# A new load path and a new step order for windowed attention with a gMLP: casting loads on one GpSimd queue, and constant matmuls in TensorE's early gaps

**Chip, cores, metric.** One core of a Trainium2 chip. The metric is the device time of one execution in microseconds (us), median of several runs; the profile gives a span that is about 2 us shorter than the time of the same execution. Engines in the profile: PE (TensorE matmul), PEld (its weight loads), DVE (VectorE), ACT (ScalarE), POOL (GpSimd), SP (SyncE); a name with a "q" is the engine's sequencer, which waits and issues. L12 is line 12 of the kernel in question, so the same step has different lines before and after.

## The reference, cut to what matters

```python
# attention: B, H, S, D = 4, 8, 768, 64; key j is kept for query i if j < 4 or 0 <= i - j < 128
scores = q @ k.T / sqrt(D);  a = softmax(where(keep, scores, -1e9));  x = heads_to_columns(a @ v)   # (4, 768, 512)
# gMLP on x: d_ff = 1024, u and v halves of 512
h = gelu_tanh(x @ w_in);  u, v = h[..., :512], h[..., 512:]
v_n = (v - mean) / sqrt(var + 1e-6) * g_ln
gated = u * (w_sg @ v_n + b_sg)            # w_sg: (768, 768), over the sequence
out = x + gated @ w_out                    # float32
```

## The kernel before

The program is one list of steps; each engine executes its own steps in that order. A step is a name with indices: `MK.0.0.2` is the mask of batch 0, head pair 0, third group of score blocks. What matters here:

```python
# loads: float32, issued from SyncE, then cast by GpSimd
def LQ(b, p):
    return nc.sync.dma_start(out=q32.new((b, p)), in_=q[b, 2*p:2*p+2].rearrange("h (p t) d -> p h (t d)", p=128))
def LV(b, p):                                   # rows of 64 floats
    return nc.sync.dma_start(out=v32.new((b, p))..., in_=v[b, 2*p:2*p+2].rearrange("h (t p) d -> p (h t) d", p=128))
def cast(dst, src):
    return nc.gpsimd.tensor_scalar(out=dst, in0=src, scalar1=1.0, scalar2=1.0, op0=ALU.mult, op1=ALU.mult)
# weights: cast by the DMA, issued from GpSimd
def LWS():
    return nc.gpsimd.dma_start(out=wsg_rows, in_=moe_w_sg.rearrange("(c p) f -> p c f", p=128))
# ... cut ...
HOLDS = "LQ.1.0<LWS LG<LWS"     # batch 1's loads wait until w_sg has landed

def transposes(name, ring, b, p):               # two heads = 128 columns in one transpose
    src = ring[b, p].rearrange("p t h d -> p t (h d)")
    ...
    for t in range(NT):
        nc.tensor.transpose(ps[:, t, :], src[:, t, :], iden)

def MK(b, p, g):                                # causal window of 128 on exp(scores)
    if g == 0 or (b == 0 and g not in MK0):
        nc.vector.tensor_mul(...)               # mask tile on VectorE
        return
    nc.gpsimd.affine_select(...)                # two selects on GpSimd
```

The steps of batch 0 end with the attention-times-v matmuls (`AV`), their normalization (`NR`), the transposes of x (`XT`, evicted by `XE`) and then the gMLP, whose first matmuls are the v-half of `x @ w_in` (`MV.0.*`). I call all that comes ahead of the first of these **the front**. After it, the gMLP of a batch and the attention of the next are interleaved.

The softmax here doesn't subtract the row's maximum and nothing guards it: scores larger than these inputs give would overflow.

## Time and profile before

| | before |
|---|---|
| time, median (range) | 173.68 us (172.44 to 173.81), 3 runs |
| span of the profile | 171.1 us |
| busy: PE, DVE, ACT, POOL | 151.1, 138.7, 101.9, 95.9 us |
| first v-half matmul starts | 33.5 us |
| w_in, w_sg, w_out have landed | 24.4, 32.0, 34.6 us |

The page's rows of digits are 40 slices of the span, each digit the busy share in tenths. "Chain" means the work that ended last, followed back from the end; each line is start, length, what. The lines themselves are in the prediction below.

### The profile page before, as it was taken

Reading aid. Unit: us, or ns where it says so; the run is one execution under the profiler, and the core shown is the slowest. Engines: PE = TensorE matmul, PEld = TensorE weight load, DVE = VectorE, ACT = ScalarE, POOL = GpSimd, SP = SyncE. Lnnn points to the kernel's source line nnn. Section 1 sums busy time; section 2 is a strip of 40 time slices with the busy share of each in tenths; the row PEclk is TensorE's granted clock in tenths of the full one; section 3 lists DMA queues with packets and bytes.
Section 4 is the critical chain, followed back from the end, with each engine's and each line's share of the span. In section 5 each row is a group of like instructions: output and inputs, shape, how many; then the busy total and the mean of one; then the engine's idle time right before and its main releaser. Section 6 shows DMA issues by size and latency. Waiting matters only on the chain.

```text
span 171.1 us, 3623 instructions
## 1 busy us (share of the span) xinstructions
PE 151.1 (88%) x1388; PEld 90.3 (53%) x1388; DVE 138.7 (81%) x290; ACT 101.9 (60%) x119; POOL 95.9 (56%) x158
## 2 busy tenths in 40 slices
PE   0447889699989899979999999999999999999970
PEld 0323568364655466645576565544565744556530
DVE  6198696629989999999999799848889994959962
ACT  0416887674995768956649985864997006860000
POOL 7789766013899999999599678043306400520000
PEclk9999999999999999999999999999999999999999
DMA  5999989999999999989999200970100374210044
GB/s 166 325 314 240 210 117 195 221 252 246 316 299 297 279 288 298 314 160 214 321 323 281 64 4 17 230 248 0 61 4 0 64 170 180 80 61 0 34 156 184
DMA packets 49617, 30.94 MB, mean 181 GB/s; under 512 B 35904, under 2 KB 46400, under 8 KB 49600
## 3 DMA queue, kind: packets, MB, share of 16 engines
q1 hardware_dynamic: 47072, 27.93, 61.5%
q0 software_dynamic: 2368, 2.75, 9.8%
q8 instruction: 11, 0.18, 0.4%
q10 hardware_dynamic: 160, 0.03, 0.1%
q14 instruction: 6, 0.05, 0.1%
HBM read 24.81 MB, written 6.29 MB: 182 GB/s over the span
## 4 chain that ended last, share of the span: by engine, by line
PE 63%; DVE 20%; ACT 5%; DMA 5%; POOL 3%; issue 2%; DVEq 0%; ACTq 0%
PE mm L466 15%; PE mm L483 11%; PE sc L446 10%; PE sc L399 10%; PE sc L310 5%; PE mm L266 4%; ACT P L318 3%; DVE qT L276 3%; DVE gtmp L471 3%; PE mm L350 3%; DVE x_sb L370 3%; DMA q<-in_q_dram 3%; DVE P L325 3%; DVE wsg_gated L476 2%; PE mm L356 2%
## 5 line engine op out<-in xcount | busy, mean ns | idle before, releaser
L318 ACT ACTIVATE P<-sc 128x1024 bf16<-128x1024 f32 (+1 forms) x48 | 43.7, 953 | 12.2 <-PE sc L310 10.6
L466 PE MATMUL mm<-wsgT,z 128*128 128x384 bf16 x192 | 34.0, 326 | 0.0
L329 POOL TENSOR_SCALAR_AFFINE_SELECT P<-P 128x512 bf16<-128x512 bf16 x28 | 20.1, 719 | 18.2 <-ACT P L318 13.8
L466 PEld LDWEIGHTS <-z 128*128 128x128 bf16 x192 | 18.0, 98 | 12.1 <-issue 1.2
L483 PE MATMUL mm<-w_out_sb,wsg_gated 128*128 128x512 bf16 x96 | 23.0, 379 | 1.1 <-DVE wsg_gated L476 1.1
L399 PE MATMUL sc<-w_in_sb,xT 128*128 128x512 bf16 x96 | 22.4, 379 | 0.2 <-ACT xT L384 0.2
L446 PE MATMUL sc<-xT,w_in_sb 128*128 128x384 bf16 x128 | 22.4, 326 | 0.0
L471 DVE SCALAR_TENSOR_TENSOR gtmp<-mm,g_sb,b_bc 128x384 bf16<-128x384 f32 x32 | 19.3, 611 | 3.6 <-PE mm L466 3.5
L487 DVE TENSOR_TENSOR ot<-mm,x_sb 128x512 f32<-128x512 f32 x24 | 16.1, 683 | 5.4 <-PE mm L483 5.3
L310 PE MATMUL sc<-qT,kT 64*128 64x256 bf16 x192 | 17.0, 287 | 3.8 <-DVE qT L276 1.7
L350 PE MATMUL mm<-v_sb,P 128*128 128x65 bf16 x192 | 18.0, 201 | 1.6 <-DVE P L325 1.4
L404 ACT ACTIVATE vt<-sc 128x1024 f32<-128x1024 f32 x12 | 12.3, 1024 | 11.7 <-PE sc L399 11.7
L182 POOL TENSOR_SCALAR q<-q 128x768 bf16<-128x768 f32 x16 | 14.3, 891 | 8.6 <-DMA q<-in_q_dram 8.6
L370 DVE TENSOR_TENSOR x_sb<-mm,rcp 128x384 bf16<-128x384 f32 x32 | 17.8, 557 | 1.1
L350 PEld LDWEIGHTS <-P 128*128 128x128 bf16 x192 | 15.2, 102 | 5.9 <-issue 2.1
L411 DVE BATCH_NORM_STATS2 st<-vt 128x6 f32<-128x512 f32 x24 | 16.2, 675 | 2.5 <-ACT vt L404 2.5
L325 DVE TENSOR_TENSOR P<-P,mask 128x1024 bf16<-128x1024 bf16 x20 | 16.4, 830 | 1.3 <-ACT P L318 1.1
L356 PE MATMUL mm<-v_sb,P 128*128 128x65 bf16 x160 | 16.9, 200 | 0.0
L446 PEld LDWEIGHTS <-w_in_sb 128*128 128x128 bf16 x128 | 12.4, 98 | 8.4
L281 ACT COPY kT<-mm 128x768 bf16<-128x768 bf16 x16 | 12.8, 801 | 5.6 <-PE mm L266 5.6
L182 POOL TENSOR_SCALAR v_sb<-v 128x768 bf16<-128x768 f32 x16 | 14.9, 937 | 1.9 <-DMA v<-in_v_dram 1.9
L418 POOL TENSOR_SCALAR rs<-mv 128x2 f32<-128x2 f32 x12 | 3.0, 251 | 22.6 <-DVE mv L412 22.2
(61 smaller groups left out, 253.8 us busy)
## 6 DMA issues: line engine op xcount, KB each, us to landing
q<-in_q_dram SPq DMA_DIRECT2D x16, 384.0 KB, 6.6
k<-in_k_dram SPq DMA_DIRECT2D x16, 384.0 KB, 5.8
v<-in_v_dram SPq DMA_DIRECT2D x16, 384.0 KB, 6.9
out_dram<-ot SPq DMA_DIRECT2D x24, 256.0 KB, 2.0
wsg_gated<-in_moe_w_sg_dram POOLq DMA_DIRECT2D x1, 1152.0 KB, 8.8
w_in_sb<-in_moe_w_in_dram POOLq DMA_DIRECT2D x2, 512.0 KB, 7.2
w_out_sb<-in_moe_w_out_dram POOLq DMA_DIRECT2D x1, 512.0 KB, 8.1
b_bc<-in_moe_b_sg_dram SPq DMA_DIRECT2D x1, 384.0 KB
```

The source lines that it names most:

```text
L182: return nc.gpsimd.tensor_scalar(out=dst, in0=src, scalar1=1.0, scalar2=1.0, op0=ALU.mult, op1=ALU.mult)
L310: nc.tensor.matmul(sc[:, hl, 256 * jl:256 * jl + n], kT[b, p][rows, 128 * j:128 * (j + 1)], qT[b, p][rows, 128 * j:128 * j + n], start=Tru ...
L318: nc.scalar.activation(out=pt[:, :, 0:w], in_=sc_ring[b, p, g][:, :, 0:w], func=AF.Exp, scale=scale)
L325: nc.vector.tensor_mul(pt[:, :, 0:w], pt[:, :, 0:w], m.unsqueeze(1).to_broadcast([128, 2, w]))
L350: nc.tensor.matmul(av[:, il, hl, :], P[b, p, i // 2][:, hl, 256 * (i % 2):256 * (i % 2) + 128], vb[:, h, i, :], start=first, stop=False)
L356: nc.tensor.matmul(av[:, il, hl, :], P[b, p, j // 2][:, hl, 256 * (j % 2) + 128:256 * (j % 2) + 256], vb[:, h, j, :], start=False, stop=False)
L370: nc.vector.tensor_mul(xs[:, 3 * half:3 * half + 3, 128 * p:128 * (p + 1)].rearrange("p t (h d) -> p t h d", h=2), av[:, :, :, 0:Dh], rcp. ...
L399: nc.tensor.matmul(hp[:, jl, :], xT[b][:, j, c, :], w_in_sb[:, c, d_half:2 * d_half], start=(c == 0), stop=(c == KD - 1))
L446: nc.tensor.matmul(hp[:, hf, 0:NH], w_in_sb[:, c, 128 * dc:128 * (dc + 1)], xT[b][:, 3 * hf:3 * hf + 3, c, :], start=(c == 0), stop=(c == ...
L466: nc.tensor.matmul(ps[:, 0:NH], z[b][:, si, 128 * dc:128 * (dc + 1)], wsgT[:, si, NH * hf:NH * (hf + 1)], start=(si == 0), stop=(si == NT ...
L471: nc.vector.scalar_tensor_tensor(out=gtmp.new((b, hf, dc)), in0=mm_ring["g", b, hf, dc][:, 0:NH], scalar=g_sb[:, dc:dc + 1], in1=b_bc[:, N ...
L483: nc.tensor.matmul(ps, gatedT[:, (2 * b + hf) % 3, dc, 128 * tl:128 * (tl + 1)], w_out_sb[:, dc, :], start=(dc == 0), stop=(dc == KU - 1))
```

## The change

Its intent: take the casts of q and k from GpSimd by letting the DMA cast them, put the large loads, all but the very first of q and k, in one queue in the order of need (so that SyncE's hold goes), keep TensorE's clock up in the front, and spread the evictions, masks and products anew over the engines. The core of the diff, cut:

```diff
-    def LQ(b, p):
-        return nc.sync.dma_start(out=q32.new((b, p)), ...)
+    def load(ring, src, b, i):                       # bfloat16 destination: the DMA casts
+        n = 2 if b == 0 else 4                       # heads per load
+        ...
+        return nc.gpsimd.dma_start(out=dst, in_=src[b, hs].rearrange("h (p t) d -> p h (t d)", p=128))
+    def rows(eng, ring, src, b, p):                  # v, float32
+        return eng.dma_start(out=ring.new((b, p))..., in_=src[b, 2*p:2*p+2]...)
     def LV(b, p):
-        return nc.sync.dma_start(...)
+        return rows(nc.sync if b in DT else nc.gpsimd, v32, v, b, p)      # DT = ()
-HOLDS = "LQ.1.0<LWS LG<LWS"
+HOLDS = "LG<LWS"
+    def HM(n):                                       # n constant matmuls ahead of the next PSUM tile's use
+        pre[0] = n
+    def fresh(ring, key):
+        t = ring.new(key)
+        for _ in range(pre[0]):
+            nc.tensor.matmul(..., iden, ks_sink[1][:, 0:512], start=True, stop=True)
     for t in range(NT):
-        nc.tensor.transpose(ps[:, t, :], src[:, t, :], iden)
+        for hl in range(2):                          # heads apart: 64 columns each
+            nc.tensor.transpose(ps[64*hl:64*hl+64, t, :], src[:, 2*(p % 2) + hl, t, :], iden)
     # batched sinks: four strips of 32 columns instead of four accumulating matmuls of 128
+        nc.tensor.matmul(ps[ks_w*p:ks_w*(p+1), :], ks[:, c0:c0+ks_w], qT[b, p][:, 256:768], start=True, stop=True)
```

... cut: the engine of each cast, eviction, mask, product and normalization is now written in the step (`.A` ScalarE, `.D` VectorE, `.P` GpSimd), and the list of steps is a new one. The end of batch 0's attention, with loads of batch 1 (`LV.1.*`) among the steps:

```text
... EX.0.0.2 HM.2 QK.0.3.2 LV.1.2 MK.0.3.0 AV.0.2.1 EX.0.3.2 MK.0.2.0 LV.1.3
SX.0.3 MK.0.3.2.D HM.3 AV.0.3.0 NR.0.2.1 MK.0.0.2.P AV.0.3.1 NR.0.3.0 AV.0.2.0 LQ.2.0 AV.0.0.1 ...
```

The x transposes of batch 0 are still made by TensorE, those of batches 1 to 3 by DMA, as before.

## The prediction

> **What bounds the kernel now.** I read the page's busy table and slices first, then the chain in order of time, then the waits of the DMA queue, then sums by stretch. Busy table and slices of the kernel before (a slice is 4.28 us, a digit is the busy share in tenths):
>
> ```profile
> PE 151.1 (88%) x1388; PEld 90.3 (53%) x1388; DVE 138.7 (81%) x290; ACT 101.9 (60%) x119; POOL 95.9 (56%) x158
> PE   0447889699989899979999999999999999999970
> PEclk9999999999999999999999999999999999999999
> DMA  5999989999999999989999200970100374210044
> ```
>
> TensorE is dense from the eighth slice on (about 34 us) and thin before; the DMA engines are full from the second slice to about 90 us. Busy times of matmuls overlap, so I take what a matmul really occupies from the chain in order of time (start, length, what):
>
> ```profile
> 13.73 0.64 PE mm L266 x6
> 20.42 0.85 PE mm L296 x2
> 101.40 0.67 PE mm L266 x12
> 108.58 0.86 PE mm L296 x4
> 119.03 5.20 PE sc L446 x32
> 143.37 3.45 PE sc L399 x16
> 152.88 6.83 PE mm L466 x42
> ```
>
> Late in the kernel a 128-column transpose (L266) occupies 0.67/12 = 56 ns, a 512-column matmul 3.45/16 = 216 ns, a 384-column one 162.5 ns. At 13.7 and 20.4 us the same transposes and sink matmuls take 107 and 425 ns: twice as long. The PEclk row does not show it, but TensorE runs at half speed early; durations change over near 27 us.
>
> With start-to-start times of the trace for the rest (a pair of 64-row, 256-column score matmuls 106 ns, an attention-times-v matmul 29.5 ns, 56 ns with the sinks) TensorE's whole work is: 320 x 0.1625 = 52.0 (L466, L446), 192 x 0.216 = 41.5 (L399, L483), 252 transposes x 0.056 = 14.1, sinks 16 x 0.216 = 3.5, scores 160 x 0.053 + 32 x 0.027 = 9.3, attention times v 352 x 0.0295 + 64 x 0.056 = 14.0: **134.4 us** of a span of 171.1. Of these 123.0 us lie after 34.5 us, where the gMLP of batch 0 begins, and take 132.6 us: 9.6 us lost, 5.6 of it between 45 and 80 us. The other 11.4 us of work are spread over the first 34.5 us. So there are two parts: **a front of 34.5 us that TensorE does not bound, and 132.6 us that it nearly does**. Sums by stretch (busy PE, PEld, DVE, ACT, POOL) show who else is full:
>
> ```profile
> 20.00:34.00 14.00, 11.84 (x157) 8.67 (x155) 10.97 (x24) 10.72 (x15) 6.83 (x10) 1.00 1.06 177
> 50.00:75.00 25.00, 23.53 (x295) 14.95 (x292) 24.50 (x47) 18.18 (x23) 24.77 (x35) 1.00 1.10 285
> 110.00:140.00 30.00, 30.00 (x262) 17.24 (x261) 24.89 (x58) 17.22 (x20) 10.16 (x20) 1.00 0.31 71
> ```
>
> From 50 to 75 us VectorE (24.5 of 25) and GpSimd (24.8) are full and TensorE loses its few microseconds; after 80 us TensorE alone is full. In the front three things meet: ScalarE's work of batch 0 (8 x 1.02 + 4 x 0.81 exp, 4 x 0.60 sink exp, 4 x 0.80 and 4 x 0.83 copies = 20.3 us from the first exp at 11.2 us), the cold TensorE, and the loads. The waits of the DMA queue carry the last:
>
> ```profile
> SPq L172 <- DMA wsg_gated<-in_moe_w_sg_dram: 16.8, 1, 16.8
> SPq L172 <- POOL q L182: 5.5, 3, 2.5
> ```
>
> SyncE holds batch 1's loads 16.8 us until the spatial weights have landed. In the trace batch 0's q and k have landed at 13.3 us, v at 19.7, w_in at 24.4, w_sg at 32.0, w_out at 34.6 us, with a hole near 24 us.
>
> **What the Trainium skill says.** "TensorE: Matmul & The Clock Gate", "What's actually happening": the clock is at half rate by default and full after a busy window of about 3.4 us. The trace agrees with the two rates (107 against 56 ns), and shows that scattered work kept it cold until about 27 us. "TensorEngine Tiling (Array Packing)", "Key Properties": different tiles run in parallel, a change of tiling mode drains the array. The trace agrees for row tiles (pairs start 3 ns apart, 8 score matmuls in 0.49 to 0.54 us against 4 x 0.106); no run yet shows column tiles, which the change brings; the page's "Restrictions" add that column tiling gives up the fast weight load. "DMA: Bandwidth & Descriptors", "Issuing engines are not separate DMA queues": all issuers share 16 engines, so one queue moves no more bytes per microsecond; the DMA row at 9 agrees. "SBUF — State Buffer", "SBUF: two separate sides": a GpSimd DMA can starve while VectorE works in a two-port mode. Four such DMAs took 0.77 to 0.87 us on GpSimd here and show no starving, but 38 of them are a different load.
>
> **The change part by part.**
>
> *GpSimd.* The casts go: 16 x (0.89 + 0.89 + 0.94) = 43.5 us out. In: 34 more DMA issues x 0.85 = 29 us (estimate; v has more rows per load than any weight and may take longer), 5 casts of v 4.7. Mask pairs fall from 28 to 19: -9 x 1.25 = -11; products move from VectorE: 15 x about 0.7 = +11 (estimate); the norm's power 8 for 12 and its small companions gone: -7. Net about -16 of 95.9 us. None of that is on the end path after 80 us; between 40 and 75 us it shortens the norm's chain and the wait for casts.
>
> *VectorE.* Evictions of q and k 16 to 11 (-5 x 0.94 = -4.7), products 32 to 17 (-7.2), full masks 20 to 29 (+9 x 0.75 = +6.8), 6 casts of v (about +3), fills, small norm operations and wider sinks (+4): about +2 on 138.7, no relief.
>
> *ScalarE.* 21 evictions for 16 (+4), 5 casts of v and one of q (+5), one x copy less: about +8 on 101.9. In batch 0 it has 21 us instead of 20.3: it still sets a floor of 21 us after the first exp.
>
> *TensorE.* q and k transposes go from 192 of 128 columns of weights to 384 of 64. If the two column halves run side by side as the row halves do, they cost no more than a drain, about 0.05 us x 24 groups of batches 1 to 3 = +1.2; if not, 24 x 6 x 0.056 = +8.1. I take +2.5. Batched sink matmuls (12 x 0.216 = 2.6) now write four strips of 32: side by side they save 1.9. The 30 constant matmuls cost 30 x 0.216 = 6.5 us warm or 12.8 cold, but lie in a front with 34.5 - 11.4 us of room; they should bring the full clock some 15 us earlier, which halves the 7.3 us of work (14.6 us cold) before 27.5 us.
>
> *The front.* Half of q and k arrives already cast, in the order of need, so the first exp comes about 1 us earlier (10 against 11.2); then ScalarE's 21 us with less waiting for the cold TensorE put its end near 32. The loads say the same: 4.7 MB of batch 0, w_in and w_sg pass at the rate of before, but without the hole: w_sg near 30 to 31, not 32.0. The new order transposes three blocks of w_sg before the first v-half matmul, so that matmul can't come before about 32; but 1 us of transposes is then already done. Gain of the front: 34.5 - 32 + 1 = **about 3.5 us**.
>
> *The rest.* 123.0 - 1.0 + 2.5 - 1.9 = 122.6 us of work; of the 9.6 us lost I expect 2.5 back, since batch 1's loads start behind w_out at once, without SyncE's hold, and the casts are gone from the path; VectorE, still full, keeps the rest. 122.6 + 7.1 = 129.7. The tail from the last matmul to the end was 171.1 - 167.1 = 4.0 and stays. Span: 32 + 129.7 + 4.0 = 165.7 us. The median time lay 2.6 over the span of the profile (173.7 against 171.1; the profiled run itself 1.9), so **168 us**.
>
> **The rivals.**
> *Column transposes are serial:* +5.5 us where TensorE is full, 173 or so: no change. For it: the weights lose the fast load; against: the row pairs overlap.
> *GpSimd's queue becomes the wait:* a DMA issue that waits for a buffer, or a long list of 256-byte rows, blocks masks and products behind it. For it: 38 issues in one in-order queue, VectorE 97% full where the lock would bite. Against: GpSimd falls to about half busy. It would cost 3 to 8 us: 171 to 176.
> *The front is bound by bytes alone:* then clock and casts are hidden anyway, the gain is 1 to 2 us: 170.
> *The order of steps is simply better:* most of the 9.6 us lost comes back, and the warm front ends before 31: 162 to 164.
>
> **Range and chances.** A sum of 168 with an error of 2 to 4 us from the transposes, 2 from the front, 2 from the losses: about 4 together. The two rivals against outweigh the one for slightly, but a schedule made afresh for this layout speaks for gain. 80%: 162.5 to 173. Faster by over 2% means under 170.2: 0.71; within 2%: 0.25; slower: 0.04.
>
> **What would show it.** Right: score and sink matmuls at full speed by about 12 us; first v-half matmul near 32; w_sg landed by 31; a q or k transpose group of 12 in under 0.45 us; batched sinks near 0.25 us; GpSimd near 80 us; TensorE's loss after the front about 7 us. Wrong: groups of 0.67 us; a GpSimd DMA issue far over 1 us, with ScalarE or TensorE waiting for masks; the first v-half matmul still at 34; VectorE's waits grown between 45 and 80 us.

## The result

The changed kernel took **178.00 us** (median of 4 runs, 177.76 to 178.75) against 173.06 us (172.34 to 173.81, 4 runs) of the kernel before on the same chip. The ratio is 1.029, 95% interval 1.023 to 1.036: slower. (Ratios are the mean time of one kernel's fast runs over that of the other's of the same rounds, so not quite the ratio of the medians quoted.) The prediction was 168.0 with a range of 162.5 to 173.0: wrong in direction and outside its range.

The page of the changed kernel, busy table and slices:

```profile
span 176.3 us, 4007 instructions
...
PE 157.0 (89%) x1610; PEld 91.0 (52%) x1610; DVE 138.6 (79%) x308; ACT 108.5 (62%) x129; POOL 83.0 (47%) x114
...
PE   0997976199999599899999999999999999999990
...
PEclk9999999759999999999999999999999999999999
...
DMA  5999999999969997848990000492300095310044
```

TensorE now starts early (second slice 9, it was 4), but the eighth slice, 31 to 35 us, is 1; and the clock row falls to 7 and 5 in the eighth and ninth. GpSimd does less than before, as intended. What happened around 31 us is in the chain in order of time, from 28 us on:

```profile
15.56 16.55 DMA w_out_sb<-in_moe_w_out_dram
...
32.68 1.02 POOL v L198
...
33.71 0.66 POOL P L376
...
34.41 0.24 PE mm L397
...
35.25 1.92 PE mm L425 x18
37.17 1.92 PE mm L493 x18
39.09 1.11 PE sc L441 x4
```

Read it from the top: the landing of w_out, at 32.1 us, lets GpSimd issue a load of v (L198); behind that load GpSimd does a mask (L376), which the last attention-times-v matmuls of batch 0 need (L397); then 36 transposes, 107 ns each, and at last the v-half of the gMLP (L441). A load of weights for the end of the gMLP has no business in that chain. GpSimd's own instructions in order of time show why it is there:

```profile
20.87 1.09 POOL L198 DMA_DIRECT2D v<-in_v_dram  x1
21.95 0.78 POOL L195 DMA_DIRECT2D q<-in_q_dram  x1
24.09 0.75 POOL L195 DMA_DIRECT2D k<-in_k_dram  x1 [1.36 <-PE mm L425]
30.58 1.04 POOL L198 DMA_DIRECT2D v<-in_v_dram  x1 [5.73 <-DMA wsg_gated<-in_moe_w_sg_dram]
32.68 1.02 POOL L198 DMA_DIRECT2D v<-in_v_dram  x1 [1.06 <-DMA w_out_sb<-in_moe_w_out_dram]
33.71 0.65 POOL L376 TENSOR_SCALAR_AFFINE_SELECT P<-P 128x512 bf16<-128x512 bf16 x1
```

The brackets hold the idle time ahead and what ended it. Two loads of v, `LV.1.2` and `LV.1.3`, wait for the landing of **w_sg and w_out**, loads that have nothing to do with v. Count the DMAs that GpSimd has issued: w_sg is the 13th and w_out the 14th; the two v loads are the 21st and 22nd. Each waits for the one eight issues before. (So do the next two: the 23rd and 24th went out at 35.5 and 37.4 us, 0.3 us after the landings of the 15th and 16th.) `MK.0.0.2.P` stands behind both in GpSimd's queue, and TensorE behind the mask. In the list of waits:

```profile
POOL v L198 <- DMA wsg_gated<-in_moe_w_sg_dram: 5.7, 1, 5.7
...
PE mm L397 <- POOL P L376: 4.2, 1, 4.2
```

Those 4.2 us (30.2 to 34.4) are one wait of TensorE. The first v-half matmuls in TensorE's list, the kernel before and then the changed one:

```profile
33.49 0.81 PE L399 MATMUL sc<-w_in_sb,xT 128*128 128x512 bf16 x3
38.89 3.47 PE L441 MATMUL sc<-w_in_sb,xT 128*128 128x512 bf16 x14
```

Where the time lies in all:

| | predicted | before | after |
|---|---|---|---|
| first v-half matmul | 32 us | 33.5 us | 38.9 us |
| from there to the last matmul's start | 129.7 us (to its end) | 133.3 us | 132.5 us |
| from the last matmul's start to the end (the tail) | 4.0 us (from its end) | 4.3 us | 5.0 us |
| span | 165.7 us | 171.1 us | 176.3 us |

So from the front to the last matmul the changed kernel is 0.8 us faster than before, and the tail takes 0.7 us of that back; in the front it is 5.4 us slower.

### The profile page after: what moved, and what is told of

The parts are those of the page before. It is cut to its first block, busy times and chain, and to the rows that moved or that the text cites. A ratio compares the mean times of both kernels' runs of the same rounds, so it can differ in the third digit from the quotient of the medians.

```text
span 176.3 us, 4007 instructions
## 1 busy us (share of the span) xinstructions
PE 157.0 (89%) x1610; PEld 91.0 (52%) x1610; DVE 138.6 (79%) x308; ACT 108.5 (62%) x129; POOL 83.0 (47%) x114
## 4 chain that ended last, share of the span: by engine, by line
PE 65%; DMA 13%; DVE 8%; POOL 7%; ACT 4%; issue 1%; DVEq 0%; POOLq 0%
PE mm L501 15%; PE sc L441 12%; PE mm L518 11%; PE sc L481 10%; DMA w_out_sb<-in_moe_w_out_dram 9%; PE sc L357 4%; DVE P L372 3%; PE mm L307 3%; PE mm L397 3%; DMA q<-in_q_dram 3%; POOL v L198 2%; PE mm L403 2%; PE mm L493 2%; PE mm L407 2%; DMA out_dram<-ot 1%
## 5 line engine op out<-in xcount | busy, mean ns | idle before, releaser
L506 DVE SCALAR_TENSOR_TENSOR gtmp<-mm,g_sb,b_bc 128x384 bf16<-128x384 f32 x32 | 19.3, 613 | 5.2 <-PE mm L501 5.1
L518 PE MATMUL mm<-w_out_sb,wsg_gated 128*128 128x512 bf16 x96 | 23.2, 379 | 0.0
L376 POOL TENSOR_SCALAR_AFFINE_SELECT P<-P 128x512 bf16<-128x512 bf16 x19 | 12.9, 682 | 21.0 <-ACT P L365 20.7
L441 PE MATMUL sc<-w_in_sb,xT 128*128 128x512 bf16 x96 | 22.6, 382 | 0.0
L462 POOL TENSOR_TENSOR rs<-rs,neg_half 128x4 f32<-128x4 f32 (+1 forms) x8 | 7.3, 907 | 31.7 <-DVE rs L457 29.1
L372 DVE TENSOR_TENSOR P<-P,mask 128x1024 bf16<-128x1024 bf16 (+1 forms) x29 | 21.1, 749 | 1.0 <-ACT P L365 0.6
L198 POOL DMA_DIRECT2D v<-in_v_dram x16 | 17.2, 1076 | 8.9 <-DMA wsg_gated<-in_moe_w_sg_dram 5.7
L397 PE MATMUL mm<-v_sb,P 128*128 128x65 bf16 x192 | 16.8, 195 | 5.1 <-POOL P L376 4.2
L511 POOL TENSOR_TENSOR wsg_gated<-gtmp,uT 128x384 bf16<-128x384 bf16 x15 | 14.0, 938 | 15.6 <-DVE gtmp L506 15.5
L397 PEld LDWEIGHTS <-P 128*128 128x128 bf16 x192 | 14.7, 98 | 9.5 <-POOL P L376 4.4
L357 PE MATMUL sc<-qT,kT 64*128 64x256 bf16 x192 | 15.9, 264 | 1.6 <-DVE kT L222 0.9
L486 ACT ACTIVATE uT<-sc 128x768 bf16<-128x768 f32 x16 | 12.8, 807 | 5.5 <-PE sc L481 5.4
L403 PE MATMUL mm<-v_sb,P 128*128 128x65 bf16 x160 | 15.9, 195 | 0.0
```

The lines of the kernel that those rows point to most:

```text
L198: return eng.dma_start(out=ring.new((b, p)).rearrange("p h t d -> p (h t) d"), in_=src[b, 2 * p:2 * p + 2].rearrange("h (t p) d -> p (h t) ...
L357: nc.tensor.matmul(sc[:, hl, 256 * jl:256 * jl + n], kT[b, p][rows, 128 * j:128 * (j + 1)], qT[b, p][rows, 128 * j:128 * j + n], start=Tru ...
L372: nc.vector.tensor_mul(pt[:, :, 0:w], pt[:, :, 0:w], m.unsqueeze(1).to_broadcast([128, 2, w]))
L397: nc.tensor.matmul(av[:, il, hl, :], P[b, p, i // 2][:, hl, 256 * (i % 2):256 * (i % 2) + 128], vb[:, h, i, :], start=first, stop=False)
L403: nc.tensor.matmul(av[:, il, hl, :], P[b, p, j // 2][:, hl, 256 * (j % 2) + 128:256 * (j % 2) + 256], vb[:, h, j, :], start=False, stop=False)
L441: nc.tensor.matmul(hp[:, jl, :], xT[b][:, j, c, :], w_in_sb[:, c, d_half:2 * d_half], start=(c == 0), stop=(c == KD - 1))
```

## The experiments

**My theory (A):** GpSimd's queue is in order and lets eight of its DMAs be in flight; two early loads stop it, and a mask behind them stops TensorE. It predicts that moving either the loads or the mask gives the loss back. **Rivals:** the mask itself is slow or late (B); the loads or w_sg bound the front in any case (C); the wait of the v loads is for a free staging buffer (A2, against A's own reading, the wait for landings, which the expectation of experiment 3 calls A1).

**1. The loads behind the mask** (`loads_behind_mask`)

```diff
- ... QK.0.3.2 LV.1.2 MK.0.3.0 AV.0.2.1 EX.0.3.2 MK.0.2.0 LV.1.3 SX.0.3 ... MK.0.0.2.P AV.0.3.1
+ ... QK.0.3.2 MK.0.3.0 AV.0.2.1 EX.0.3.2 MK.0.2.0 SX.0.3 ... MK.0.0.2.P LV.1.2 LV.1.3 AV.0.3.1
```

> Edit: the two v loads of batch 1 that stood ahead of the last GpSimd mask of batch 0 are issued behind it; nothing else. Theory A (GpSimd's in-order queue: those two issues wait for w_sg and w_out to land, and the mask waits behind them): TensorE's 4.2 us stall before the last attention-times-v matmuls goes, the transposes after it run warm (56 ns, not 107), the first v-half matmul comes at 33 to 34 us instead of 39.1, the span falls by 5 to 6 us to about 171. Rival B (GpSimd's mask itself is late or slow): no change, the stall stays at 3 us or more. Rival C (batch 1's data or w_sg bound the front): the stall goes but TensorE waits elsewhere for a load, the span falls by under 2 us.

Measured: 172.21 us, ratio to before 0.996 (0.991 to 1.001), span 170.5, first v-half matmul at 33.0 us. GpSimd in order of time:

```profile
25.92 0.67 POOL L376 TENSOR_SCALAR_AFFINE_SELECT P<-P 128x512 bf16<-128x512 bf16 x1 [0.16 <-ACT P L365]
...
30.76 1.06 POOL L198 DMA_DIRECT2D v<-in_v_dram  x1 [3.35 <-DMA wsg_gated<-in_moe_w_sg_dram]
33.16 1.02 POOL L198 DMA_DIRECT2D v<-in_v_dram  x1 [1.34 <-DMA w_out_sb<-in_moe_w_out_dram]
```

The mask now runs at 25.9 us. The loads wait as long as ever, but nobody stands behind them. 5.8 us of span are back. B and C fall.

**2. The mask on VectorE** (`mask_on_vector`)

```diff
- MK.0.0.2.P
+ MK.0.0.2.D
```

> Edit: the one last mask of batch 0 goes from GpSimd to VectorE, the loads stay where they were. Theory A: the same gain as with the loads moved, 5 to 6 us, within 1 us of it, although GpSimd still stands still from about 25 to 32 us. Rival C (late loads): less than half of that gain, as the loads are not issued any earlier than before.

Measured: 172.42 us, ratio 0.997 (0.992 to 1.002), span 170.8, first v-half matmul at 33.6 us. Within 0.3 us of the first experiment, although the loads were issued no earlier than in the changed kernel (30.9 and 33.1 us, there 30.6 and 32.7). The loss was the mask's wait, not late data.

**3. Which wait is it?** (`v32_six`, one look)

```diff
-    v32 = Ring("v32", 4, [128, 2, NT, Dh], F32)
+    v32 = Ring("v32", 6, [128, 2, NT, Dh], F32)
```

> Edit: the changed kernel with six v staging buffers instead of four. Which wait blocks GpSimd? Theory A1 (the GpSimd DMA queue waits for the landing of the DMA eight issues before, w_sg and w_out): the two v issues still go out right after w_sg and w_out land (30 to 33 us), the stall stays near 4 us and the first v-half matmul at 39. Rival A2 (they wait for a free staging buffer): both go out near 26 us, the stall goes.

Measured: one time, 179.31 us, state unknown; first v-half matmul at 38.9 us. GpSimd in order of time:

```profile
31.26 1.04 POOL L198 DMA_DIRECT2D v<-in_v_dram  x1 [5.28 <-DMA wsg_gated<-in_moe_w_sg_dram]
33.40 1.02 POOL L198 DMA_DIRECT2D v<-in_v_dram  x1 [1.10 <-DMA w_out_sb<-in_moe_w_out_dram]
```

With buffers to spare the same two issues wait for the same two landings. A2 falls.

**4. The two loads from SyncE** (`two_loads_on_sync`)

```diff
-        return rows(nc.sync if b in DT else nc.gpsimd, v32, v, b, p)
+        return rows(nc.sync if b in DT or (b, p) in ((1, 2), (1, 3)) else nc.gpsimd, v32, v, b, p)
```

> Edit: the changed kernel, the order of steps untouched, but the two v loads that blocked GpSimd are issued from SyncE. Theory A (one in-order GpSimd queue for all loads is what costs): the mask runs near 26 us, the first v-half matmul comes at about 33, the span falls by 5 to 6 us, as when the loads moved behind the mask. If the two loads now overtake w_sg on the 16 DMA engines, w_sg lands up to 2.5 us later (two loads of 384 KB) and the gain is 3 to 4 us.

Measured: 171.78 us, ratio 0.995 (0.992 to 0.998), span 169.9, first v-half matmul at 32.9 us. w_sg landed at 31.1 us, 1 us later than in experiment 1, but that did not show in the first v-half matmul. This run also counts the queue for us. GpSimd in order of time:

```profile
25.83 1.09 POOL L376 TENSOR_SCALAR_AFFINE_SELECT P<-P 128x512 bf16<-128x512 bf16 x1 [0.41 <-ACT P L365]
...
31.36 0.76 POOL L195 DMA_DIRECT2D q<-in_q_dram  x1 [3.67 <-DMA wsg_gated<-in_moe_w_sg_dram]
35.08 0.75 POOL L195 DMA_DIRECT2D k<-in_k_dram  x1 [2.96 <-DMA w_out_sb<-in_moe_w_out_dram]
```

With two loads taken out of the queue, the waits for w_sg and w_out have moved on to the next two, loads of q and k of batch 2, which are now the 21st and 22nd. The wait goes with the place in the queue and not with what is loaded.

The kept traces also say where the eight comes from. In the operands of the DMA instructions, which the views do not print, GpSimd's DMAs report their landings on eight semaphores in turn (numbers 99 to 106). In the changed kernel w_sg reports on 103 and w_out on 104; the 21st and 22nd issues report on the same two again, and wait for them first. In this experiment the two loads of batch 2 do so. It is thus the program, as it was built, that holds such an issue until the landing eight issues earlier; whether the chip has a limit of its own no run shows.

**5. Work for TensorE during the stall** (`fill_the_stall`)

```diff
- AV.0.0.1
+ HM.20 AV.0.0.1
```

> Edit: 20 more constant matmuls (20 x 0.216 = 4.3 us at full clock) ahead of the last attention-times-v matmuls of batch 0, so that TensorE works through the stall. The result is unchanged as a start flag overwrites them. Theory A with its second part (the stall of 4.2 us let the clock fall to half, which costs 18 + 18 transposes 51 ns each and some of the first v-half matmuls, 2.1 us in all): the stall's end stays at 34.4 us, but the 36 transposes take 2.0 instead of 3.8 us, the span falls by 1.5 to 2.2 us. Rival (the slow transposes wait for something else, such as their evictions): they stay at 107 ns, no gain, or a loss.

Measured: 176.95 us, ratio 1.022 (1.016 to 1.029), span 175.3; the clock row has no dip. The direction is right, the size is half: 1.0 us of span (its four executions have spans of 174.7 to 175.3 us, those of the changed kernel 176.0 to 177.0; the intervals of the two ratios overlap). The 36 transposes took 2.8 us instead of 3.8, not 2.0: once the clock is full they wait for ScalarE's evictions of x, and the stall itself ended 0.4 us later (34.8). So of the 5.8 us, some 1 us is the half clock that the stall left behind, the rest is the wait.

**6. Six output buffers** (`six_out_buffers`)

```diff
-    ot = Ring("ot", 3, [128, d_model], F32)
+    ot = Ring("ot", 6, [128, d_model], F32)
```

> Edit: six output buffers instead of three. Theory A's third part (the last three residual sums wait for the landing of stores three back, since the new order leaves six output tiles to the end): the tail from the last matmul to the end falls from 7.1 to about 5.5 us or less, the span by 1 to 2 us. Rival: the tail is the stores themselves, and nothing changes.

A miss. I had read the last residual sums, which do wait for earlier stores in the changed kernel, as part of the tail; 177.55 us, ratio 1.028 (1.021 to 1.035), span 176.2. With six buffers the waits for stores are gone, but the last sum starts at 171.97 us instead of 172.04: it waits for TensorE's last matmul, which had only been hidden by the other wait. I had also taken 7.1 us for that tail, from a chain that leaves TensorE before its end; the last matmul starts at 171.3 us, and the tail is 5.0 us.

**7. No constant matmuls** (`unblocked_no_constants`): experiment 1's kernel with all `HM` steps taken out.

> Edit: the kernel with the loads behind the mask, and no constant matmuls at all. What are they worth once nothing blocks? Theory (they only warm a front that ScalarE and the loads bound): TensorE stays cold (107 ns a transpose) until after 20 us, yet the first v-half matmul moves by under 1.5 us from 33.0, and the time by under 1%. Rival (the clock bounds the front): the first v-half matmul comes 3 us or more later, at 36 or more, and the time rises by about 2%.

Measured: 171.18 us, ratio 0.992 (0.987 to 0.997). The clock was full from 19.2 to 26.0 us, then half again until 29.4; the first v-half matmul came at 33.6 us, and the time was, if anything, shorter than with the constants.

**8. The same with more rounds** (`unblocked_no_constants_again`)

> Repeat with more rounds: the changed kernel with the two v loads behind the mask and no constant matmuls, the fastest version so far (ratio 0.992 in three rounds). If that was real: a ratio of 0.988 to 0.996 again, clear of 1. If it was the spread between rounds: an interval that holds 1.

Measured: **170.80 us** (170.41 to 171.35, 6 runs) against 172.84, ratio 0.989 (0.985 to 0.993), span 169.6, first v-half matmul at 32.3 us, although the clock was at half again from 23.7 to 30.5 us. This version beats both kernels: the one before by 1.1%, which by a 2% rule counts as the same, and the changed one by about 4% (170.80 against 178.00, medians of different calls).

**9. The constants alone, in the kernel before** (`before_with_constants`): the `HM` step and `fresh` of the diff added to the kernel before, and 23 constant matmuls ahead of its first transposes, scores and sinks.

> Edit: the kernel before, with 23 constant matmuls put ahead of its first transposes, scores and sink matmuls (one part of the change alone). Theory (the clock does not bound the front): the clock is full by about 9 us instead of 27.5, the first v-half matmul stays within 0.7 us of 33.5 us, the time within 0.5% of before. Rival (a cold TensorE is on the path of the front, as the prediction took it): the first v-half matmul comes 1.5 us or more earlier, the time falls by 0.8% or more.

Measured: 173.10 us, ratio 0.995 (0.988 to 1.002); the profile fell on an execution marked slow, so its span is not compared. In it the clock was full from 12.5 to 19.3 us and from 22.7 on, not from 9, so my constants warmed less than I had expected; the first v-half matmul came at 33.6 us (33.5 before). No gain that is clear of zero, but with three fast executions only: the interval reaches down to 0.988 and does not by itself exclude the rival's 0.8%. It is together with 7 and 8, and with a first v-half matmul that did not move, that it speaks against the clock as what bounded the front.

**10. Both repairs together** (`sync_no_constants`): experiment 4's kernel without the constants.

> Edit: the changed kernel with the two blocking v loads issued from SyncE and without the constant matmuls: the two repairs that helped, together. Theory (the block is the whole loss, the constants are worth nothing, the rest of the kernel is as fast as before to 1 us): first v-half matmul at 33 to 34 us, rest 132 to 133 us, span 170 to 171, the time 0.5 to 1.2% under the kernel before: the same by the 2% rule. Rival (one of the two repairs needs the constants' warm clock): 172 us of span or more.

Measured: 172.07 us, ratio 0.996 (0.991 to 1.002), span 170.4. The front ended at 31.7 us, the earliest of all runs, and the rest then took 134.2 us instead of 132.5. TensorE in order of time shows why:

```profile
45.50 0.86 PE L307 MATMUL mm<-iden,q 128*64 128x128 bf16 x24 [1.54 <-DMA q<-in_q_dram]
```

Batch 1's second load of q landed at 45.5 us here and at 42.0 us in experiment 1: two v loads on a second queue shared the DMA engines with it (landed at 35.1 and 45.5 us). In experiment 4, with the same two loads on SyncE, it landed at 45.5 us too, and TensorE waited 0.6 us for it; here the front ended 1.2 us earlier and the wait is 1.5 us. What the front gained, TensorE waited for data. The expectation of a rest of 132 to 133 us was a miss.

**11. Less for VectorE from 43 to 73 us** (`vector_relief`), on experiment 1's kernel:

```diff
- CV.1.2.D CV.1.3.D MK.1.2.1.D MK.1.0.1.D
+ CV.1.2.P CV.1.3.P MK.1.2.1.P MK.1.0.1.P
```

> Edit: the kernel with the loads behind the mask, and two casts of v and two masks of batch 1 go from VectorE to GpSimd, which is 60 to 80% busy there. Theory (VectorE, full from 43 to 73 us, keeps TensorE's 6 us of loss there, which is why the rest of the kernel gained only 1 us): VectorE does about 4 us less there, TensorE's loss falls by 1 to 3 us, the span to 168 to 169. Rival (ScalarE and the chain through it bound that stretch, or GpSimd becomes late): within 1 us of 170.5, or slower.

Measured: times of 171.71 to 177.0 us in four runs, two of them slow; the profiled run is a fast one, span 171.0, rest of the kernel 132.6 us (132.5 without). VectorE's busy time in the 30 us that begin 10 us after the first v-half matmul fell from 28.9 to 26.3 us, and TensorE gained nothing.

**12. Less for ScalarE there** (`scalar_relief`), on experiment 10's kernel:

```diff
- Z.0.3.A Z.0.0.A CV.1.2.D CV.1.3.D
+ Z.0.3.D Z.0.0.D CV.1.2.P CV.1.3.P
```

> Edit: the same kernel, and in batch 0's norm the two blocks that ScalarE normalizes (0.8 us each) go to VectorE, which gives two casts of v (0.6 us each) to GpSimd. Theory (between 43 and 63 us TensorE waits for ScalarE: its row of normalize, gelu and copies stands ahead of the table load and the first exp of batch 1): that exp comes 1.2 to 1.6 us earlier after the first v-half matmul than without, TensorE's loss there falls by about 1 us, the time by 0.5 to 1%. Rival (VectorE bounds it after all): z comes later, the spatial matmuls wait, no gain or a loss of up to 1 us.

Measured: 173.27 us, ratio 1.001 (0.997 to 1.005), against 0.996 for experiment 10. The first exp of batch 1 came 17.4 us after the first v-half matmul instead of 18.2, less than expected, and the spatial matmuls then waited 1.6 us for VectorE's z. In this run w_sg also landed late, at 32.0 us, which held TensorE for 1.8 us in the front, so the loss of time is not all of the edit's making. The rival's outcome: no gain. **What bounds the stretch from 43 to 73 us stays open**: VectorE, ScalarE and the order of their steps are all close to it, and shifting single steps only moved the wait.

## Why the prediction was wrong, point by point

The predicted span was 165.7 us, the measured one 176.3: 10.6 us too little. They divide into 6.9 in the front, 2.8 in the rest and 1.0 in the tail (rounded; 0.3 of the tail is that I count from the last matmul's start here, the other 0.7 was not traced). The block in GpSimd's queue accounts for 5.8 of them. Without it (experiment 1) the span is still 4.8 us over the prediction, 1.0, 2.8 and 1.0 in the same three parts, and no faster than before by the 2% rule: the forecast gain is missed even then, for the reasons further down.

- **GpSimd's queue (the step that failed).** The prediction put it among the rivals: "a DMA issue that waits for a buffer, or a long list of 256-byte rows, blocks masks and products behind it", 3 to 8 us, and argued against it because "GpSimd falls to about half busy". That argument was wrong. GpSimd did fall to 83.0 us (near 80 was predicted), and it was idle while it blocked: an in-order queue blocks by what its head waits for. Nor was it a buffer or the rows: it was the landing of the DMA eight issues before, for which the program's own semaphores made it wait. Experiments 1, 2 and 4 each give back 5.5 to 6.4 us of span, so the rival's 3 to 8 us was a fair size; experiment 3 excludes the buffer.
- **The front otherwise.** Without the block it ends at 32.3 to 33.6 us, in experiment 10 at 31.7; predicted was 32. The prediction's reasons hold in part: w_sg landed at 29.6 us (predicted 30 to 31) and scores ran at full speed by 12 us; but the first exp, expected at 10 us, came at 11.6 (11.2 before). And the gain was overstated, as I took 34.5 us for the start of the gMLP before, where the chain enters it; the first v-half matmul was at 33.5.
- **The clock and the constants.** The constants did raise the clock at once (the trace's clock records begin at 8.7 us instead of 27.5). That this shortens the front is not borne out: taking them out cost nothing (7, 8), adding them to the kernel before gained nothing clear of zero (9). The rival that "clock and casts are hidden anyway" was right on the clock, as far as these runs show.
- **Transposes and sinks by column tiles.** The sizes were nearly right. In the chain of the changed kernel:

```profile
80.58 0.46 PE mm L307 x12
...
82.57 0.33 PE mm L343 x4
```

  Twelve transposes of 64 columns take 0.46 us where six of 128 took 0.34 (0.67/2): +0.12 x 24 = +2.9 us in batches 1 to 3, predicted +2.5. Four sink matmuls take 0.33 instead of 0.86 us: -1.6 for three batches, predicted -1.9. The halves do run side by side, but not for free.
- **The rest.** 132.5 us measured (133.3 before), 129.7 predicted. Apart from the two terms above (0.4 and 0.3) and the reading of the start (0.7), the mis-sized term is "of the 9.6 us lost I expect 2.5 back". By the same account, with 56 ns and the other slots and 38 ns for a 64-column transpose, TensorE lost 9.9 us after its first v-half matmul before and 8.8 after: 1.1 came back, 1.4 less than predicted. The sums by stretch of the changed kernel (start and end, length, then busy PE, PEld, DVE, ACT, POOL) show who was full there:

```profile
50.00:75.00 25.00, 22.28 (x321) 13.47 (x319) 24.10 (x44) 23.24 (x29) 18.68 (x22) 1.00 0.95 180
```

  In the 25 us from 50 to 75 VectorE is busy 24.1 us (24.5 before), GpSimd 18.7 (24.8) and ScalarE 23.2 (18.2). But this window is an earlier stage of the changed kernel, whose front ends 5.4 us later. Like is compared with like in experiment 1, with its front at 33.0 us: from 43 to 73 us GpSimd is busy 20.7 us there and 29.3 before, VectorE 28.9 and 29.1, ScalarE 26.3 and 24.4. So **GpSimd was relieved by 8.6 of 30 us while VectorE stayed full, and TensorE's loss fell by little**; that ScalarE took GpSimd's place is not shown (experiments 11 and 12). The prediction added 8 us to ScalarE over the whole kernel and looked at them in the front alone.
- **The estimates for GpSimd.** A v load took 1.08 us to issue (estimated 0.85, with the warning that it may be longer), a product 0.94 us (estimated 0.7). No product stands in the chain that ended last, but issues of v do, with 4.2 us (2.4% of the span). Starving, which the prediction kept open for 38 such DMAs, does not show: the longest of the issues took 1.30 us.

## What to carry to other kernels

When loads move into the queue of an engine that also computes, ask for every issue what it will wait for, the semaphore on which it will report included, and what stands behind it in that queue; the engine's busy share says nothing about this. Put no step that the critical engine waits for behind a prefetch, or issue the prefetch from an engine that only issues. And before adding work that keeps a clock up, check that the stage is bound by that engine at all: here taking out 30 constant matmuls cost nothing that the runs show.

## What the Trainium skill lacked or had wrong

- No page has it: a program that lets its GpSimd DMAs report on eight semaphores in turn can hold an issue until the landing eight issues earlier, and so stop GpSimd's computing. Here: 5.7 us idle ahead of one issue, 4.2 us of TensorE. It is shown for this program (semaphores 99 to 106 in its traces), not as a limit of the chip.
- "DMA: Bandwidth & Descriptors", "Anatomy of one DMA", calls the descriptor generation of a GpSimd DMA small and variable, and that section gives no figure for it. Here an issue occupied GpSimd for 0.75 to 0.78 us for q and k and 1.08 us for v, which comes in rows of 256 bytes. One is small; all 38 issues took 34 of GpSimd's 83 us.
- "TensorE: Matmul & The Clock Gate", "PE-mode transpose", says that the full clock does not engage for transposes and gives about 275 ns for one in a kernel. Here, in the kernel before, the record of one 128-column transpose lasts 217 to 219 ns after 80 us and mostly 314 ns in the first 20 us, and in a stream they follow each other every 56 and 107 ns: they do run at both rates. Whether they help to raise the clock no run shows.
